# A fused sparse attention and SwiGLU kernel: another order of the same steps, and 39 products on zeros in place of 88

## The chip, the core and the metric

The kernel runs on one NeuronCore of a Trainium2 chip. Five engines work side by side, each through its own queue and strictly in the order of that queue: TensorE (PE: matrix products and transposes), ScalarE (ACT: exponentials, tanh, copies out of PSUM), VectorE (DVE: elementwise work and reductions), GpSimd (POOL: casts, masks, and the issue of some transfers) and SyncE (SP: the issue of the other transfers). They meet through semaphores: an instruction waits in its queue until its inputs are there, and whatever stands behind it waits too. The metric is the time of one execution in microseconds (us).

## The reference

There are two parts. The first is attention over 4 batches, 8 heads, 768 positions and 64 features, in which each query sees only some chunks of 32 keys. For each chunk an upper bound of the score is made from the chunk's smallest and largest key; the 6 best causal chunks are kept; softmax runs over the kept keys. The second part takes the attention's rows (3072 x 512), normalizes them, and applies a gated feed-forward layer of width 1536.

```
k_min, k_max = min, max of k over each chunk
ub    = sum over features of max(q * k_min, q * k_max), causal chunks only
kept  = the 6 chunks with the largest ub, and only keys up to the query
attn  = softmax(q k^T / 8 over the kept keys) @ v
xn    = x / sqrt(mean(x^2) + 1e-6) * rms_g          # x: attn as 3072 x 512
g     = xn @ w_gate
out   = (g * sigmoid(g) * (xn @ w_val)) @ w_out
```

## The kernel before

**Pieces.** Heads are taken in pairs: 16 pairs, four to a batch (pair 0 to 3 is batch 0). The feed-forward layer is done in halves of a batch, 384 rows each, so there are 8 of them. All of it is cut into 1923 steps. A step is one to 32 instructions on one engine. Each step has a name; a text such as "the scores of pair 3" below means all steps `sc` of that pair.

**A pair's path.** SP issues the loads `kload` and `qload` (two transfers each, line 505) into the tiles `knat` and `qnat`; POOL issues the load of v (`vx`, line 481). PE turns k and q (`kT`, `qT`, line 525), three blocks a step; ACT or DVE evicts them (`kE`, `qE`, lines 297 and 301). DVE reduces the chunks (`kmn`, `kmx`, lines 554 and 556), `dif` takes the difference (line 607), `relu` clamps q (line 641 or 643). PE makes the bounds (`ub`, line 731), ACT and DVE evict them (`ubE`), PE turns them back (`up`, line 755), DVE adds the causal mask (`ubm`, line 770), finds the best chunks (`max`, line 658) and writes the selection (`sel`, lines 682 and 687, or 673 and 676 from pair 3 on). For pairs 0 to 2 the selection is turned on PE (`selT`, line 702) and copied by ACT or DVE (`selC`); from pair 3 on SP turns it by two DMA transposes (`qX`, line 565), which wait for `sel` and for a cast of q (`qN`). Casts of k to bf16 (`kC`, `qC`) run on POOL or ACT. Then come twelve scores (`sc`, lines 876 and 882), twelve exponentials on ACT (`exp`, line 893), masks on POOL (`mask`, line 899), twelve products with v (`av`, line 912) and the division on DVE (`xb`, lines 932 and 933). Pair 3 does this in two halves of its queries.

**The feed-forward part.** For each half of a batch, DVE and ACT sum the squares (`sq`), DVE and POOL take the root (`eps`, `root`), DVE scales three rows of blocks (`xs`, line 989). In batch 0 PE turns them (`tp`, line 1011) and ACT or DVE evicts (`tpE`); in later batches SP turns them (`xT`). Then follow twelve `gate` (PE, four products each, line 1045), `tanh` (ACT, line 1052), `tg` (DVE, line 1058), `val` (PE, line 1066), `hh` (DVE, line 1074), and nine `po` (PE, line 1086), whose results are evicted (`poE`) and stored by SP (`out`). The weights come in six transfers that POOL issues: `wg`, `wv` (line 445) and `wo` (line 450), two each.

**Fillers.** 88 further steps, `busy` (line 346), are products of a tile of zeros with itself, into a PSUM bank that nobody reads. 48 of them are 512 columns wide and need only the tile `zeros`, which DVE clears; 40 are 256 wide and may run after the last score of pair 2.

**What sets the order.** Nothing runs while the steps are declared: `order.add` collects them with their dependencies, the buffers that they open and a rank. `Order.run` then plays the program in the kernel's own time model, written out in the source: each engine takes, when it is free, the ready step of the lowest rank whose buffers are free. Ranks are sums of the numbers in `RANK` and `TIMES`. Fillers have the highest ranks, so they are taken where PE has nothing else. Transfers form one line of `load / RATE` each, whichever queue issues them. The order in which steps are taken is the order in which their instructions are emitted, and so the order of every queue; the slot numbers chosen there fix which PSUM bank or SBUF tile a step uses.

```
done = order.run(PLACE)
for s in done:
    s.emit(s.eng)
```

Of the kernel before, what the change touches and what calls it, by code (L numbers as in the profile page):

```python
# [11 lines left out]
ACT = mybir.ActivationFunctionType  # L12
# [13 lines left out]
RANK = (  # L26
    dict(
        av=439.71, dif=-349.0, eps=-276.35, exp=56.9, kC=119.11, kE=221.89, kT=-479.5,
        kload=-91.99, kmn=-561.73, kmx=-221.73, max=-117.69, qC=120.39, qE=644.67, qN=97.14,
        qT=303.27, qX=110.23, qload=17.43, relu=-156.64, root=392.56, sc=392.96, sel=176.91,  # L30
        selC=388.0, selT=-168.59, sq=-325.5, tp=-47.15, tpE=460.17, ub=-387.44, ubE=-1000.64,
        ubm=-238.37, up=-379.03, vload=-360.06, xb=-167.37, xs=293.02,
    ),
    dict(
        av=-243.01, dif=-122.81, eps=-968.41, exp=80.0, gate=-57.45, hh=-33.27, kC=474.21,
        kE=54.78, kT=-28.02, kload=327.35, kmn=571.37, kmx=673.95, mask=-6.85, max=351.72,
        out=-338.93, po=268.25, poE=188.61, qE=-4.14, qN=444.8, qT=271.57, qX=-691.62,
        qload=314.07, relu=202.91, root=-1348.37, sc=-186.72, sel=354.08, sq=285.76, tanh=579.3,
        tg=-259.04, ub=-101.04, ubE=-390.25, ubm=307.49, up=-117.99, val=-52.48, vload=103.56,
        xT=119.23, xb=-299.83, xs=-84.52,  # L40
    ),
)

TIMES = {
# [15 lines left out]
}  # L60


class Buf:
    def __init__(self, kind, sub=None):
        self.kind, self.sub = kind, sub
        self.users, self.slot, self.tile, self.done = 0, None, None, 0.0


class Step:
    def __init__(self, name, occ, rank, emit, deps, opens, uses, load, port):  # L70
        self.name, self.engs, self.occ = name, list(occ), occ
        self.rank, self.emit, self.load, self.port = rank, emit, load, port
        self.deps = [d for d in deps if d is not None]
        self.opens, self.bufs = list(opens), list(opens) + list(uses)
        self.start = self.seen = self.eng = None
        self.left, self.ready, self.next = 0, 0.0, []


class Order:
# [1079 lines left out]
```

## Time and profile before

| | before |
|---|---|
| median of 3 runs | 316.09 us (316.01 to 316.24) |
| the profiled execution | span 314.0 us; its own time is not listed apart from that |
| PE | 308.6 us busy, 98% of the span |
| DVE | 230.7 us, 73% |
| ACT | 194.4 us, 62% |
| POOL | 100.7 us, 32% |
| fillers (line 346) | 88 products, 1.3 to 53.6 us |
| moved by DMA | 35.36 MB, mean 113 GB/s |

Busy time is the union of an engine's instructions. A product's record also covers the stretch in which the next one already runs, so the price of one in a dense row is the distance from start to start. A window of the profile gives the busy time of each engine in a stretch of the span; the timeline gives rows "start, length, engine, line, operation, tiles, count"; the time to landing of a transfer runs from its issue to the semaphore that tells of its end.

### The profile page before, as it was taken

Reading aid. Unit: us, or ns where it says so; the run is one execution under the profiler, and the core shown is the slowest. Engines: PE = TensorE matmul, PEld = TensorE weight load, DVE = VectorE, ACT = ScalarE, POOL = GpSimd, SP = SyncE. Lnnn points to the kernel's source line nnn. Section 1 sums busy time; section 2 is a strip of 40 time slices with the busy share of each in tenths; the row PEclk is TensorE's granted clock in tenths of the full one; section 3 lists DMA queues with packets and bytes.
Section 4 is the critical chain, followed back from the end, with each engine's and each line's share of the span. In section 5 each row is a group of like instructions: output and inputs, shape, how many; then the busy total and the mean of one; then the engine's idle time right before and its main releaser. Section 6 shows DMA issues by size and latency. Waiting matters only on the chain.

```text
span 314.0 us, 7640 instructions
## 1 busy us (share of the span) xinstructions
PE 308.6 (98%) x2844; PEld 196.1 (62%) x2844; DVE 230.7 (73%) x654; ACT 194.4 (62%) x420; POOL 100.7 (32%) x157
## 2 busy tenths in 40 slices
PE   7999999999999999999999999999999999999995
PEld 4567877666566775666667565656666645655542
DVE  7699986888988487967986799879464663873530
ACT  5589987863475987478579654344988823333321
POOL 8666534342353564045357300001522220000000
PEclk9999999999999999999999999999999999999999
DMA  8999989989989898979934640002341045001102
GB/s 171 210 190 178 145 108 207 198 114 143 196 86 199 126 179 152 201 164 222 158 79 61 93 102 0 2 2 52 84 94 59 20 118 150 3 0 65 38 22 111
DMA packets 113301, 35.36 MB, mean 113 GB/s; under 512 B 106224, under 2 KB 110064, under 8 KB 113264
## 3 DMA queue, kind: packets, MB, share of 16 engines
q1 hardware_dynamic: 83152, 26.62, 40.9%
q0 software_dynamic: 28512, 7.87, 25.6%
q10 hardware_dynamic: 1600, 0.39, 0.6%
q8 instruction: 22, 0.36, 0.5%
q14 instruction: 15, 0.12, 0.1%
HBM read 28.57 MB, written 6.29 MB: 111 GB/s over the span
## 4 chain that ended last, share of the span: by engine, by line
PE 97%; DMA 1%; ACTq 0%; ACT 0%; issue 0%
PE gp L1045 20%; PE vp L1066 20%; PE po L1086 20%; PE sc L876 12%; PE av L912 7%; PE busy L346 4%; PE pq L525 4%; PE pk L525 3%; PE ub L789 2%; PE ub L731 2%; DMA qnat<-in_q_dram 1%; PE up L811 1%; PE sc L882 1%; PE up L755 1%; PE tp L1011 0%; ACTq L505 0%
## 5 line engine op out<-in xcount | busy, mean ns | idle before, releaser
L893 ACT ACTIVATE pt<-sc 128x512 bf16<-128x512 f32 (+2 forms) x192 | 88.4, 578 | 10.1 <-PE sc L876 5.3
L1052 ACT ACTIVATE sg<-gp 128x384 bf16<-128x384 f32 x96 | 47.7, 500 | 62.7 <-PE gp L1045 60.0
L1066 PE MATMUL vp<-xT,wv 128*128 128x384 bf16 x384 | 77.0, 326 | 0.0
L1045 PE MATMUL gp<-xT,wg 128*128 128x384 bf16 x384 | 76.2, 326 | 0.0
L1086 PE MATMUL po<-wo,hh 128*128 128x512 bf16 x288 | 69.3, 379 | 0.0
L1058 DVE SCALAR_TENSOR_TENSOR tg<-sg,gp 128x384 bf16<-128x384 bf16 x96 | 52.2, 548 | 21.7 <-ACT sg L1052 19.5
L1074 DVE TENSOR_TENSOR hh<-vp,tg 128x384 bf16<-128x384 f32 x96 | 51.8, 551 | 11.1 <-PE vp L1066 7.3
L1045 PEld LDWEIGHTS <-wg 128*128 128x128 bf16 x384 | 36.8, 98 | 24.5 <-issue 1.0
L1066 PEld LDWEIGHTS <-wv 128*128 128x128 bf16 x384 | 36.9, 98 | 24.1
L876 PE MATMUL sc<-qs,ke 128*128 128x128 bf16 (+5 forms) x420 | 51.4, 251 | 0.0
L1086 PEld LDWEIGHTS <-hh 128*128 128x128 bf16 x288 | 27.6, 98 | 27.5
L301 POOL CAST ke<-kt 64x768 bf16<-64x768 f32 x31 | 26.4, 852 | 36.9 <-ACT kt L297 17.0
L876 PEld LDWEIGHTS <-ke 128*128 128x128 bf16 (+1 forms) x420 | 30.3, 97 | 11.3 <-issue 1.6
L899 POOL TENSOR_SCALAR_AFFINE_SELECT pt<-pt 128x512 bf16<-128x512 bf16 (+1 forms) x48 | 24.4, 527 | 37.6 <-ACT pt L893 37.4
L912 PEld LDWEIGHTS <-pt 128*128 128x128 bf16 x672 | 28.8, 98 | 7.7 <-POOL ke L301 0.6
L912 PE MATMUL av<-vx,pt 128*128 128x65 bf16 x672 | 32.6, 193 | 0.0
L299 ACT ACTIVATE osb<-po 128x512 f32<-128x512 f32 x19 | 11.4, 602 | 21.4 <-PE po L1086 21.4
L346 PE MATMUL busy<-zeros 128*128 128x512 bf16 (+1 forms) x88 | 20.1, 349 | 1.3 <-DVE zeros L341 1.3
L933 DVE TENSOR_TENSOR xb<-av,rden 128x384 bf16<-128x384 f32 (+1 forms) x34 | 18.1, 534 | 1.2
L989 DVE SCALAR_TENSOR_TENSOR xs<-xb,ri,gains 128x512 bf16<-128x512 bf16 x24 | 16.9, 746 | 2.7 <-DMA xT<-xs 2.1
L301 POOL CAST qn<-qnat 128x768 bf16<-128x768 f32 x10 | 8.2, 821 | 31.9 <-DMA qs<-qn 30.7
L481 POOL DMA_DIRECT2D vx<-in_v_dram x16 | 16.8, 1052 | 4.0 <-PE av L912 2.6
(87 smaller groups left out, 303.1 us busy)
## 6 DMA issues: line engine op xcount, KB each, us to landing
out_dram<-osb SPq DMA_DIRECT2D x24, 256.0 KB, 2.2
knat<-in_k_dram SPq DMA_DIRECT2D x30, 192.0 KB, 4.3
qnat<-in_q_dram SPq DMA_DIRECT2D x30, 192.0 KB, 4.8
vx<-in_v_dram POOLq DMA_DIRECT2D x16, 192.0 KB, 4.7
wg<-in_moe_w_gate_dram POOLq DMA_DIRECT2D x2, 768.0 KB, 8.6
wv<-in_moe_w_val_dram POOLq DMA_DIRECT2D x2, 768.0 KB, 7.8
wo<-in_moe_w_out_dram POOLq DMA_DIRECT2D x2, 768.0 KB, 9.9
qs<-qn SPq DMA_TRANSPOSE x26, 3.3
```

The lines of the kernel that those rows point to most:

```text
L301: engine[e].tensor_copy(out_, in_)
L346: nc.tensor.matmul(t[:, 0:n], zeros[:, 0:P], zeros[:, 0:n], start=True, stop=True)
L876: nc.tensor.matmul(t[:, x:x + m, :].rearrange("p a b -> p (a b)"), ke[kk, kb * P:(kb + 1) * P], qs[kk, q0 * P:(q0 + m) * P], start=not tri ...
L893: nc.scalar.activation(out=t[:, 0:nn, :], in_=sc.tile[:, 0:nn, :], func=ACT.Exp, scale=SCALE)
L899: nc.gpsimd.affine_select(out=pt.tile[:, 0:nd, :], in_=pt.tile[:, 0:nd, :], compare_op=ALU.is_ge, fill=0.0, base=0, pattern=[[0, nd], [1, ...
L912: nc.tensor.matmul(av.tile[:, qi - i0, :], pt.tile[:, x, :], VX[c.v.slot][:, hl * NT + kb, :], start=(begin and m == 0), stop=(left[0] == ...
L1045: nc.tensor.matmul(t[:], wg[:, g, hs], XT[b].tile[:, g, cols], start=(g == 0), stop=(g == NP - 1))
L1052: nc.scalar.activation(out=t[:], in_=gp.tile[:], func=ACT.Tanh, scale=0.5)
L1058: nc.vector.scalar_tensor_tensor(out=t[:], in0=sg.tile[:], scalar=1.0, in1=gp.tile[:], op0=ALU.add, op1=ALU.mult)
L1066: nc.tensor.matmul(t[:], wv[:, g, hs], XT[b].tile[:, g, cols], start=(g == 0), stop=(g == NP - 1))
L1074: nc.vector.tensor_tensor(out=t[:], in0=vp.tile[:], in1=tg.tile[:], op=ALU.mult)
L1086: nc.tensor.matmul(po.tile[:], hhs[ht].tile[:, th * P:(th + 1) * P], wo[:, ht, :], start=(ht == 0), stop=(ht == NHT - 1))
```

## The change

The planner is gone. `PROGRAM`, a string of 1874 words, holds the order instead. In each word the letter is the engine (P, A, D, G for POOL, S), the number is the step in the order of declaration, and the numbers behind the colon are the slots of the buffers that the step opens. `Order.run` reads the words. Steps, tiles, buffers, instructions and arithmetic stay as they were, except for three things: the order within every queue; the engine of steps that may run on two (for instance `selC` of pair 0, from ACT to DVE, and a `kC` and `qC` of pair 0); and the fillers: of the 88 steps the string holds the first 39 (numbers 4 to 42), all 512 wide.

```
-RANK = ( ... )
-TIMES = { ... }
+PROGRAM = (
+    "D59 G0 D3 S82:0 P4:0 A2 D1 G64 P5:1 D52 S81 D53 D54 D55 P6:2 G61 G65 S88:1 P7:3 S87 P8:4 G60 G66 S152:2 P9:5 "
+    "P10:6 G67 P85:7 S157:3 G73 P83:0 D86:0 P11:1 P12:2 G71 A84 D95:0 P91:3 D58 S326:4 P13:4 P14:5 A92:1 D57 "
...
+    "S224:0 D110:0 G113:0 P334:4 D330:6 A171:0 P111:7 A328 D172 P332:1 A335:2 D112 P173:3 G339:2 A99 S399:1 P25:5 "
...
+)
-    def run(self, places):
+    def run(self, program):
+        engines = {"P": "PE", "A": "ACT", "D": "DVE", "G": "POOL", "S": "SP"}
         out = []
-        while len(out) < len(self.steps):
...
+        for word in program.split():
+            n, _, slots = word[1:].partition(":")
+            s = self.steps[int(n)]
+            s.eng = engines[word[0]]
+            new = [b for b in s.opens if b.slot is None]
+            for b, x in zip(new, slots.split(",") if slots else (), strict=True):
+                b.slot = int(x)
+            out.append(s)
         return out
...
-    done = order.run(PLACE)
+    done = order.run(PROGRAM)
```

What moves, read from the two orders queue by queue, as far as the prediction speaks of it:

- PE before the first `gate`: the same steps in both (48 `sc`, 48 `av`, 14 `qT`, 12 `kT`, 5 `ub`, 5 `up`, 3 `selT`, 3 `tp`), and 88 fillers before, 39 after. 24 of the 39 stand ahead of the first score. No filler stands behind the first `gate` in either.
- PE from the first `gate` to `kT` of pair 5: before 9 `gate`, 4 `val`, 12 `sc`; after 8 `gate`, 3 `val`, 6 `sc`, 2 `tp`.
- DVE: the clearing of one tile `qn` (step 59) stands ahead of the clearing of `zeros` (step 3). `sel` of pair 4 stood ahead of the squares of batch 0's first half; now it stands behind the three `xs` and behind `eps` of the second half.
- ACT before the first `tanh`: before 9 `qE`, 5 `kE`, 5 `ubE`, 3 `tpE`, 1 `selC`, 1 `qC`; after 12, 6, 4, 2, 0, 0. The rest is the same (48 `exp`, 5 `relu`, 4 `sq`, `ke0`, one `kC`). The third `sq` of batch 0's second half stands between `tpE` and `tanh`, and `eps` of that half waits for it.
- SP: the gains' load moves from ahead of pair 1's loads to behind `qX` of pair 3. Around pair 4: `qX` of pair 4 (twice), then `kload` of pair 5, `qload` and `kload` of pair 7, in both orders.
- POOL: before, v of pairs 0, 1, 3, 2, then `wg`, `wv`, a `root`, `wg`, a `root`, `wv`, v of pair 4. After, v of pairs 0, 1, 3, 6, 2, then `wg`, `wg`, `wv`, the two `root`, v of pair 4, `wv`, v of pair 7, `wo`.

More of the change, by code (lines that the diff above doesn't have):

```diff
@@ L22 @@
 GUARD = 480.0
[L26 to L41, printed above, removed]
-)
-TIMES = {
[15 rows of a table removed]
-}
+PROGRAM = (
[123 rows of a table added]
+)
 class Buf:
@@ L65, in __init__ @@
         self.kind, self.sub = kind, sub
-        self.users, self.slot, self.tile, self.done = 0, None, None, 0.0
+        self.users, self.slot, self.tile = 0, None, None
 class Step:
@@ L74, in __init__ @@
         self.opens, self.bufs = list(opens), list(opens) + list(uses)
-        self.start = self.seen = self.eng = None
-        self.left, self.ready, self.next = 0, 0.0, []
+        self.eng = None
 class Order:
-    RATE = 0.21e6
-    COLD = 4.5
-    TAIL = {"PE": 0.27, "ACT": 0.18, "DVE": 0.14, "POOL": 0.10, "SP": 2.0}
     def __init__(self, slots, limits):
@@ L261, in rank @@
         return r
-    PLACE = {"": 1.0}
-    for i, kinds in enumerate(RANK):
-        for kind, x in kinds.items():
-            PLACE[f"{kind}.{i}"] = x
     const = ctx.enter_context(tc.tile_pool(name="const", bufs=1))
@@ L1124 @@
             ffn(b, half, f"f{b}.{half}", f"pacef{b}.{half}")
-    PLACE.update(TIMES)
-    done = order.run(PLACE)
+    done = order.run(PROGRAM)
     for s in done:
```

95 lines of the change are left out of this document (removed), and 135 rows, old and new, of tables (PROGRAM, TIMES).

## The prediction

> **What bounds the kernel now.** I read the page first: busy shares, slices, and the group of the fillers.
>
> ```profile
> span 314.0 us, 7640 instructions
> ...
> PE 308.6 (98%) x2844; PEld 196.1 (62%) x2844; DVE 230.7 (73%) x654; ACT 194.4 (62%) x420; POOL 100.7 (32%) x157
> ...
> PE   7999999999999999999999999999999999999995
> ...
> PEclk9999999999999999999999999999999999999999
> DMA  8999989989989898979934640002341045001102
> GB/s 171 210 190 178 145 108 207 198 114 143 196 86 199 126 179 152 201 164 222 158 79 61 93 102 0 2 2 52 84 94 59 20 118 150 3 0 65 38 22 111
> ...
> L346 PE MATMUL busy<-zeros 128*128 128x512 bf16 (+1 forms) x88 | 20.1, 349 | 1.3 <-DVE zeros L341 1.3
> ```
>
> PE is never idle. So its queue sets the end, and time goes only if PE gets less to do, or if what it does not do in the first 54 us is not replaced by a wait. PE's waits and the windows of all engines (columns: PE, PEld, DVE, ACT, POOL busy, PEclk, DMA share, GB/s) say how tight that is.
>
> ```profile
> PE busy L346 <- DVE zeros L341: 1.3, 1, 1.3
> PE pq L525 <- DMA qnat<-in_q_dram: 0.3, 1, 0.3
> ```
>
> ```profile
> 5.00:20.00 15.00, 14.66 (x133) 8.77 (x132) 11.59 (x32) 10.37 (x18) 10.81 (x17) 1.00 1.09 208
> 20.00:48.00 28.00, 27.97 (x427) 21.52 (x426) 26.43 (x103) 26.73 (x62) 13.61 (x18) 1.00 1.16 147
> 48.00:54.00 6.00, 6.00 (x68) 4.91 (x66) 4.32 (x11) 4.56 (x12) 2.82 (x4) 1.00 1.19 219
> 54.00:314.00 260.00, 256.23 (x2216) 159.16 (x2214) 184.97 (x500) 151.25 (x329) 69.24 (x104) 1.00 0.59 100
> ```
>
> From 20 to 48 us ACT is busy for 26.73 of 28 and DVE for 26.43: the fillers there cover waits for these two. Ahead of 20 and behind 48 ACT has holes. Behind 54 us PE alone is full.
>
> **The first part: what the fillers cost.** The timeline of PE gives their spacing.
>
> ```profile
> 1.26 2.74 PE L346 MATMUL busy<-zeros 128*128 128x512 bf16 x6 [1.26 <-DVE zeros L341]
> ...
> 19.34 0.43 PE L876 MATMUL sc<-qs,ke 128*128 128x128 bf16 x3
> ...
> 49.77 0.71 PE L346 MATMUL busy<-zeros 128*128 128x256 bf16 x5
> 50.32 0.82 PE L525 MATMUL pq<-ident_f,qnat 128*128 128x128 f32 x6
> ...
> 52.73 1.24 PE L346 MATMUL busy<-zeros 128*128 128x512 bf16 x5
> 53.81 1.46 PE L1045 MATMUL gp<-xT,wg 128*128 128x384 bf16 x8
> ...
> 64.57 0.82 PE L525 MATMUL pk<-ident_f,knat 128*128 128x128 f32 x6
> 65.23 1.46 PE L1045 MATMUL gp<-xT,wg 128*128 128x384 bf16 x8
> 66.53 0.81 PE L1066 MATMUL vp<-xT,wv 128*128 128x384 bf16 x4
> ...
> 307.69 2.54 PE L1086 MATMUL po<-wo,hh 128*128 128x512 bf16 x11
> ```
>
> Five narrow ones take 50.32 - 49.77 = 0.55, or 0.11 us each; five wide ones 53.81 - 52.73 = 1.08, or 0.216 each; the first six at the start stand 0.42 apart (the next instruction starts at 3.79). The change drops 40 narrow (4.4 us) and 9 wide (1.9 us): 6.3 us. Against that, one more `qn` tile is cleared ahead of `zeros`:
>
> ```profile
> 2.52 1.75 DVE L356 MEMSET qn<- 128x896 uint32 x2
> ```
>
> That is 0.8 us by which the first product starts later. If nothing else waits, the first `gate` moves from 53.81 to 53.81 - 6.3 + 0.8 = 48.3. The work behind the first `gate` is the same set of steps, and PE does it without a hole: from 53.81 to 307.69 + 2.54 = 310.23, 256.4 us. The last stretch to the end of the span is 314.0 - 310.2 = 3.8 us (last eviction and store, the same steps). So the end is the time of the first `gate`, plus 256.4, plus PE's new waits behind it, plus 3.8.
>
> **Can ACT and DVE keep up?** ACT first. Up to the first `tanh`, 0.85 us behind the first `gate`, it is busy for 10.37 + 26.73 + 4.56 = 41.7 us.
>
> ```profile
> 9.22 0.84 ACT L297 ACTIVATE qs<-qt 64x768 bf16<-64x768 f32 x1
> 10.77 0.38 ACT L297 ACTIVATE ubs<-ub 96x256 f32<-96x256 f32 x1 [0.71 <-PE ub L731]
> ...
> 12.60 0.87 ACT L297 ACTIVATE qt<-pq 128x384 f32<-128x384 f32 x2 [0.90 <-PE pq L525]
> ...
> 17.67 1.62 ACT L297 ACTIVATE qs<-st 64x768 bf16<-64x768 bf16 x2 [0.17 <-PE st L702]
> 19.19 0.85 ACT L297 ACTIVATE qt<-pq 128x384 f32<-128x384 f32 x2
> 19.93 0.75 ACT L893 ACTIVATE pt<-sc 128x128 bf16<-128x128 f32 x2
> ```
>
> The new order takes from it `selC` (1.62), `qC` (0.84), one `ubE` (0.38) and one `tpE` (about 0.5), and gives it four evictions (0.44 each): 41.7 - 3.3 + 1.7 = 40.1 us. So a `tanh` 5.5 us earlier, at 49.1, leaves ACT from its first eviction (about 5.7) 43.4 us for 40.1 us of work. Before it had 49.
>
> The early stretch decides. The first score starts at 19.34 now, right behind the 1.62 us of `selC` on ACT. In the new order that copy runs on DVE beside ACT; the last thing in front of the scores is then pair 0's cast on ACT, behind `ke0`, `ubE` and two evictions. I put their rows end to end from PE's first transposes (about 5.0, seven cold fillers behind 2.05) and come to 17.4 for the first score, an estimate. From the first `exp` (19.93) to the first `tanh` ACT now has 31.4 us of work and takes 34.7; the new list there is about as long, 31.5. Without any hole the `tanh` comes at 17.5 + 31.5 = 49.0 and the first `gate` at 48.2, where PE alone would put it (48.3). With the hole of 20 to 48 us (28.00 - 26.73 = 1.3) the gate comes at 49.5; with that of 48 to 54 as well (6.00 - 4.56 = 1.4) at 50.9. I take 49.5: the second hole is the tail in which batch 0's norm waits on its own chain, and the new order has two evictions and a `relu` of pair 5 there.
>
> DVE gives a second bound. Its work up to the third `xs` is the 11.59 + 26.43 of the windows and the part of 48 to 54 that ends with this row, and it loses about what it gains (a `max` pair, a `sel` and a `qN` go behind; a `selC`, a `ubE` come in front).
>
> ```profile
> 45.10 0.45 DVE L673 SCALAR_TENSOR_TENSOR qn<-m,ubm 128x288 bf16<-128x288 f32 x1
> 45.47 0.19 DVE L676 TENSOR_SCALAR qn<-m 128x12 bf16<-128x12 f32 x1
> ...
> 50.13 2.07 DVE L989 SCALAR_TENSOR_TENSOR xs<-xb,ri,gains 128x512 bf16<-128x512 bf16 x3
> ```
>
> Some 43 us of work that can start at 0.9 and must stand about 3 us while the first transposes come end no earlier than 47; a transpose and an eviction later it is 48. So PE, ACT and DVE would all be full at once: 48.3 is a floor, not a forecast.
>
> **A wait that takes the place: pair 5's keys.** `sel` of pair 4 stood at 45.10 to 45.66, eight microseconds ahead of the gate. It moves behind `xs` and behind `eps`, which waits for the last `sq`, and so ends some 1.3 us behind the gate. SP issues two transposes of its result, and pair 5's keys queue behind them:
>
> ```profile
> 45.81 3.44 SPq L565 DMA_TRANSPOSE qs<-qn  x2
> 49.30 2.78 SPq L505 DMA_DIRECT2D knat<-in_k_dram  x2
> ```
>
> ```profile
> DMA to landing us min/median/max: 7.4/8.8/10.1
> ```
>
> ```profile
> knat<-in_k_dram SPq DMA_DIRECT2D x30, 192.0 KB, 4.3
> ```
>
> The third row is the time to landing in the window 49 to 52 us, the two transfers of pair 5's keys; the last one is the page's median of all. With the gate at G the transposes issue at G + 1.4, the keys 49.30 - 45.81 = 3.5 later at G + 4.9, the second of the two about 0.7 behind. By the median both are there at G + 9.9; as slow as in the window (the second 10.1 behind its issue) at G + 15.7. PE wants them after 8 `gate` and 3 `val` (two gates take 66.53 - 65.23 = 1.30, so 11 x 0.65), 6 scores and 2 `tp` (about 0.22 each, as a 512-column product), at G + 9.0. Before, the same keys were wanted at 64.57, 10.8 behind the gate. So the wait is between nothing (a load faster than the median) and 6.7 us; the median gives 0.9. I take 1.5, near the median, because the weight load beside which the slow one ran has gone earlier.
>
> ```profile
> 49.24 0.80 POOL L445 DMA_DIRECT2D wg<-in_moe_w_gate_dram  x1
> ```
>
> The new order issues it before the two `root`; what then runs beside the keys is v of pair 4, the second `wv` and v of pair 7.
>
> The Trainium skill, DMA: Bandwidth & Descriptors, section "Issuing engines are not separate DMA queues", says that transfers begun by different engines end up on the same 16 DMA engines and interleave. The trace agrees: the keys took up to 10.1 us beside `wg`, 4.3 as a rule. By that rule POOL's three transfers would slow pair 5's keys again, and the sum would be that of the fourth case below; by the median row it is the forecast.
>
> **The sum.** 49.5 + 256.4 + 1.5 + 3.8 = 311.2 us of span. The median of the runs, 316.09, lies 2.1 above the span; so 313.3 us, 0.9% below. Other moves (gains later, v of pair 6 earlier, the finer mix of `sc`, `av`, `gate`) I cost at nothing: the cover is feed-forward work, and in 54 to 314 ACT is busy for 151 of 260 us and DVE for 185. Where that cover is gone, a wait is paid in full, since PE takes its queue in order.
>
> **The other cases.** What a measurement tells from no change here is about 0.2%, 0.6 us.
>
> First, all three engines stay full and the keys come in time: 48.3 + 256.4 + 3.8 + 2.1 = 310.6. For it: the waits of PE above are 1.6 us in all. Against it: the holes in ACT's windows. 0.2.
>
> Second, the forecast, with 0.7 to 3 us of wait: 312 to 315. 0.35.
>
> Third, the gate comes late, ACT losing what it loses now (50.9, or 52 where early loads are late too): 314.7 to 316. This is also the case in which the change does not do what it says, since the zeros go and PE stands idle in their place. 0.17, half of it within 0.2%.
>
> Fourth, slower: the transposes of pair 4 hold up pair 5's keys, which take as long as in the window 49 to 52. PE waits 6.7 us: 49.5 + 256.4 + 6.7 + 3.8 + 2.1 = 318.5. It decides once the wait is over 53.8 - 49.5 = 4.3 us, that is, once these keys land later than 53.8 + 9.0 = 62.8 us. For it: both slow rows. Against it: the `wg` beside it is gone. 0.23.
>
> Fifth, such a wait slows the clock as well. At the start products stand 0.42 apart instead of 0.216 for about 3.4 us, although PE is busy; as many again would cost 8 x 0.2 = 1.6 us: 320.1. The Trainium skill, TensorE: Matmul & The Clock Gate, section "What's actually happening", has the clock halved after an idle window of about 3.4 us; PEclk shows nothing of it here, since PE is never idle that long. 0.05.
>
> So faster 0.62 (the first two and a part of the third), same 0.1, slower 0.28. The range is 310.0 to 318.5: from PE's sum with the gate some 0.6 earlier to the fourth case. The forecast's own range is 312 to 315.
>
> **What would show it.** In the profile after: the first `gp` row at 49.5 (48.3 to 51); `busy` x39 and about 10 us; the first `sc` row near 17.4; ACT busy for over 27 of 28 us in 20 to 48; a wait of PE on `pk` for the DMA of `knat` near 59 us, of 1 to 3 us; no other wait over 1 us behind it; `po` ending 3.8 us ahead of the span's end. I am wrong on the covers if PE's waits behind 70 us come to more than 1.5 us; wrong on ACT if the gate comes behind 51; wrong on the sign if pair 5's keys land behind 62.8.

## The result: 343.8 us in place of 316.05, and the profile after

The changed kernel takes 343.79 us (median of 4 runs, 342.98 to 345.49) against 316.05 us for the kernel before on the same chip. The ratio is 1.088, with a 95% interval of 1.086 to 1.091. The forecast was 313.3 with a range up to 318.5, so size and sign are both wrong. Times in this document are medians of all executions, ratios and intervals leave out those more than 1.5% above the kernel's fastest, and a profile shows one execution, whose time is given where it lies far from the median. In the rows of the changed kernel the line numbers are 8 lower: `busy` is line 338, the loads 497, the transposes 517, `sc` 868, `gate` 1037; in the runs further below they are 7 to 10 lower.

The page: its span, the busy time of the engines, and the granted clock in 40 slices.

```profile
span 341.7 us, 7415 instructions
...
PE 310.9 (91%) x2770; PEld 196.8 (58%) x2795; DVE 231.7 (68%) x661; ACT 188.8 (55%) x410; POOL 103.3 (30%) x160
...
PEclk9899996797899999999999999999989999999998
```

PE has 49 weight loads (PEld) fewer, one for each product on zeros that is gone; its own count falls by 74 because some 25 records of products are missing from this trace. PE is busy for 91% of the span in place of 98%. The clock, full throughout before, falls in four stretches: near 9 to 17, 51 to 68, 77 to 94 and 247 to 256 us. The timeline of PE has the first `gate`:

```profile
66.63 1.62 PE L1037 MATMUL gp<-xT,wg 128*128 128x384 bf16 x9
```

It stands 12.8 us later than before (53.81); the way from there to the span's end is 275.1 us in place of 260.2. So of the 27.7 us, 12.8 arise ahead of the `gate` and 14.9 behind it. PE's waits (total, times, longest, in us) name the causes:

```profile
PE pq L517 <- DMA qnat<-in_q_dram: 8.6, 3, 7.9
PE pk L517 <- DMA knat<-in_k_dram: 7.2, 2, 4.3
PE av L904 <- POOL pt L891: 3.2, 1, 3.2
PE busy L338 <- DVE zeros L333: 2.2, 1, 2.2
PE av L904 <- DMA vx<-in_v_dram: 1.6, 1, 1.6
```

Before there was one wait for a load, of 0.3 us. The chain of work that ended last, in order of time, holds transfers too. Three of its pieces, the keys of pair 1, the last load of pair 0's queries and a load of pair 5's queries:

```profile
3.43 3.71 DMA knat<-in_k_dram
7.16 4.99 DMA qnat<-in_q_dram
37.89 19.68 DMA qnat<-in_q_dram
```

The third, 19.7 us for half of one pair's queries, is twice the slowest landing that the prediction reckoned with (10.1). Before the change this load and the first weight transfer (`wg`) went out so, first SP, then POOL:

```profile
33.50 2.19 SPq L505 DMA_DIRECT2D qnat<-in_q_dram  x2
38.53 0.79 POOL L445 DMA_DIRECT2D wg<-in_moe_w_gate_dram  x1
```

The queries landed 4.0 to 4.7 us behind their issues, when the first weights set out, and PE wanted them at 50.32. After the change three weight transfers stand around the load, and PE waits:

```profile
36.81 1.51 POOL L437 DMA_DIRECT2D wg<-in_moe_w_gate_dram  x2
37.47 0.97 SPq L497 DMA_DIRECT2D qnat<-in_q_dram  x2
39.96 0.75 POOL L437 DMA_DIRECT2D wv<-in_moe_w_val_dram  x1
57.71 0.87 PE L517 MATMUL pq<-ident_f,qnat 128*128 128x128 f32 x3 [7.88 <-DMA qnat<-in_q_dram]
```

The windows (columns as in the prediction) show the clock beside the waits:

```profile
5.00:20.00 15.00, 11.60 (x100) 6.91 (x98) 9.28 (x29) 6.61 (x12) 9.05 (x17) 0.89 1.22 224
20.00:48.00 28.00, 25.35 (x381) 19.38 (x383) 25.34 (x85) 25.45 (x58) 18.39 (x24) 1.00 1.23 142
48.00:68.00 20.00, 11.90 (x105) 8.26 (x103) 8.73 (x34) 9.56 (x22) 1.79 (x3) 0.74 0.47 82
68.00:100.00 32.00, 25.93 (x217) 17.19 (x216) 20.04 (x47) 15.58 (x34) 13.09 (x19) 0.89 1.17 162
```

PE is idle for 3.4 of 15, 8.1 of 20 and 6.1 of 32 us, and the clock is 0.89, 0.74 and 0.89 there. Of the 8.1 us, 7.9 are the one wait for pair 5's queries.

Two more places can be read from the timelines. The first is the start. The second halves of pair 0's four loads are issued not by SP but by ACT (line 505, after the change 497). ACT's timeline before and after:

```profile
0.80 1.07 ACTq L505 DMA_DIRECT2D knat<-in_k_dram  x2
1.90 1.05 ACTq L505 DMA_DIRECT2D qnat<-in_q_dram  x2
2.98 1.28 ACT L338 ACT_TABLE_LOAD   x1 [2.98 <-issue]
```

```profile
0.80 0.49 ACTq L497 DMA_DIRECT2D knat<-in_k_dram  x1
1.32 1.28 ACT L330 ACT_TABLE_LOAD   x1 [1.32 <-PEq L1134]
2.61 0.20 ACT L330 ACTIVATE first<-ident_f 128x1 f32<-128x1 f32 x1
4.70 0.40 ACTq L497 DMA_DIRECT2D knat<-in_k_dram  x1
5.14 2.39 ACTq L497 DMA_DIRECT2D qnat<-in_q_dram  x2
```

The word `A2` (`first`, the activation that brings ACT's table) stands ahead of three of the four. Before, the four went out between 0.80 and 2.95 us; now the last goes out at 7.16. `first` itself takes only 1.5 us of that. In the chain the last issue stands right behind the landing of pair 1's keys (3.43 + 3.71 = 7.14), so the rest looks like a wait for earlier transfers; why ACT's issue should hang on them was not looked into. The second place is POOL's queue near the end:

```profile
242.01 0.66 POOL L891 TENSOR_SCALAR_AFFINE_SELECT pt<-pt 128x512 bf16<-128x512 bf16 x1
248.65 0.83 POOL L293 CAST qn<-qnat 128x768 bf16<-128x768 f32 x1 [5.98 <-issue]
249.42 0.42 POOL L891 TENSOR_SCALAR_AFFINE_SELECT pt<-pt 128x256 bf16<-128x256 bf16 x1
```

A mask of pair 12 stands behind a cast of pair 15 (`qN`). The profile names no releaser for the 5.98 us before the cast; the cast's buffer is one that DMA transposes read, and the last of these, issued at 241.3, lands 7.1 us later, just before the cast starts. PE waits 3.2 us for the mask.

### The profile page after: what moved, and what is told of

Its sections match the earlier page's. It is cut to its first block, busy times and chain, and to the rows that moved or that the text cites. A ratio compares the mean times of both kernels' runs of the same rounds, so it can differ in the third digit from the quotient of the medians.

```text
span 341.7 us, 7415 instructions
## 1 busy us (share of the span) xinstructions
PE 310.9 (91%) x2770; PEld 196.8 (58%) x2795; DVE 231.7 (68%) x661; ACT 188.8 (55%) x410; POOL 103.3 (30%) x160
## 4 chain that ended last, share of the span: by engine, by line
PE 75%; DMA 12%; DVE 3%; issue 3%; SPq 2%; POOL 2%; ACT 0%; POOLq 0%
PE po L1078 18%; PE vp L1058 17%; PE gp L1037 17%; DMA qnat<-in_q_dram 11%; PE sc L868 8%; PE av L904 5%; PE pq L517 3%; PE pk L517 2%; SPq L497 2%; PE ub L781 2%; PE busy L338 1%; DMA knat<-in_k_dram 1%; DVE m L650 1%; POOL ke L293 1%; PE up L803 1%
## 5 line engine op out<-in xcount | busy, mean ns | idle before, releaser
L885 ACT ACTIVATE pt<-sc 128x512 bf16<-128x512 f32 (+1 forms) x192 | 92.9, 556 | 38.8 <-PE sc L868 36.1
L1037 PE MATMUL gp<-xT,wg 128*128 128x384 bf16 x384 | 73.4, 329 | 0.0
L1066 DVE TENSOR_TENSOR hh<-vp,tg 128x384 bf16<-128x384 f32 x96 | 51.1, 552 | 12.6 <-PE vp L1058 11.5
L868 PE MATMUL sc<-qs,ke 89*128 89x128 bf16 (+5 forms) x419 | 56.3, 255 | 1.8 <-DVE hh L1066 1.5
L904 PE MATMUL av<-vx,pt 128*128 128x65 bf16 x672 | 40.9, 197 | 4.8 <-POOL pt L891 3.2
L904 PEld LDWEIGHTS <-pt 128*128 128x128 bf16 x672 | 35.0, 100 | 16.4 <-POOL pt L891 3.5
L891 POOL TENSOR_SCALAR_AFFINE_SELECT pt<-pt 128x256 bf16<-128x256 bf16 (+1 forms) x48 | 25.0, 531 | 58.6 <-ACT pt L885 54.6
L868 PEld LDWEIGHTS <-ke 89*128 89x128 bf16 (+1 forms) x420 | 31.0, 99 | 12.1 <-issue 3.7
L293 POOL CAST ke<-kt 64x768 bf16<-64x768 f32 x31 | 25.8, 831 | 18.2 <-PE sc L868 10.1
L517 PE MATMUL pq<-ident_f,qnat 128*128 128x128 f32 x96 | 16.4, 292 | 8.6 <-DMA qnat<-in_q_dram 8.6
L517 PE MATMUL pk<-ident_f,knat 128*128 128x128 f32 x96 | 16.6, 292 | 7.3 <-DMA knat<-in_k_dram 7.2
L924 DVE RECIPROCAL rden<-av 128x6 f32<-128x6 f32 (+1 forms) x34 | 6.9, 202 | 21.0 <-PE av L904 20.7
## 6 DMA issues: line engine op xcount, KB each, us to landing
wo<-in_moe_w_out_dram POOLq DMA_DIRECT2D x2, 768.0 KB, 10.1
```

The lines of the kernel that those rows point to most:

```text
L293: engine[e].tensor_copy(out_, in_)
L517: nc.tensor.transpose(t[:, j * P:(j + 1) * P], nat[w].tile[:, j0 + j].rearrange("p h d -> p (h d)"), ident_f[:])
L868: nc.tensor.matmul(t[:, x:x + m, :].rearrange("p a b -> p (a b)"), ke[kk, kb * P:(kb + 1) * P], qs[kk, q0 * P:(q0 + m) * P], start=not tri ...
L885: nc.scalar.activation(out=t[:, 0:nn, :], in_=sc.tile[:, 0:nn, :], func=ACT.Exp, scale=SCALE)
L891: nc.gpsimd.affine_select(out=pt.tile[:, 0:nd, :], in_=pt.tile[:, 0:nd, :], compare_op=ALU.is_ge, fill=0.0, base=0, pattern=[[0, nd], [1, ...
L904: nc.tensor.matmul(av.tile[:, qi - i0, :], pt.tile[:, x, :], VX[c.v.slot][:, hl * NT + kb, :], start=(begin and m == 0), stop=(left[0] == ...
```

## The experiments

Three theories. **Late loads:** transfers are issued late, or starved beside POOL's weights, and each wait costs its length and some clock behind it. **Fewer products on zeros:** with 39 in place of 88, TensorE has too little to do, and its clock falls of itself. **Many small waits:** the finely mixed order costs a little everywhere. All runs compare with the kernel before on the same chip (315.9 to 316.1).

### One cause at a time in the changed kernel

`first` behind all four of pair 0's loads:

```diff
-D59 G0 D3 S82:0 P4:0 A2 D1 G64 ... S88:1 P7:3 S87 P8:4
+D59 G0 D3 S82:0 P4:0 D1 G64 ... S88:1 P7:3 S87 A2 P8:4
```

> The changed kernel (343.8) with one word moved: ScalarE's `first` (the activation that brings its table) stands behind all four of pair 0's loads that ScalarE issues, as before the change, not ahead of three of them. Late loads (each wait on TensorE for a transfer that was issued late or starved is the cause): the four are issued by 3 us and land by 7 in place of 12.1, the second half of `kT@a0` starts near 5 in place of 8.8, `sc` starts near 18 in place of 21.8, and the time falls by 3 to 5 us, to 338.8 to 340.8; the wait of 8 us for pair 5's queries stays. Fewer products on zeros (the clock falls because TensorE has too little to do): the number of products is the same, so 343 to 345. Many small waits of the finely mixed order: 342 to 344, at most 2 us.

Measured: 332.25 us, four executions from 327.69 to 336.41, ratio 1.043 (1.037 to 1.049). By the median that is 11.5 us less than the changed kernel, by the ratio (329.3 us) 14.5: more than twice what was expected. The profile is of an execution of 333.62 us. Its waits and one window:

```profile
PE pk L515 <- DMA knat<-in_k_dram: 6.5, 2, 5.5
PE pq L515 <- DMA qnat<-in_q_dram: 4.5, 3, 4.0
```

```profile
48.00:68.00 20.00, 16.79 (x135) 11.10 (x136) 12.41 (x38) 12.69 (x27) 8.03 (x11) 0.91 0.70 106
```

The first score starts at 17.82 in place of 21.77, so 4 us come back at the start, as expected. But the wait for pair 5's queries, which was expected to stay, halves (7.9 to 4.0): all goes 4 us earlier, these queries are issued at 33.5 and take 16.1 us in place of 20.1 from the first issue to the last landing. The clock between 48 and 68 rises from 0.74 to 0.91 with it. The first `gate` stands at 57.46, 9.2 us earlier, of which 4.0 arise before the first score and 3.9 at this wait. In this profile a late start cost its own length and as much again.

Pair 5's queries right behind pair 4's:

```diff
-... S539:4 A121:2 ... P540:5 S469:6 P214 ...
+... S539:4 S469:6 A121:2 ... P540:5 P214 ...
```

> The changed kernel (343.8) with one word moved: the load of pair 5's queries stands on SyncE right behind the load of pair 4's (S539), ahead of the three weight transfers of GpSimd's queue in place of beside them. Late loads: it lands 10 us earlier or more, the wait of 8.0 us at `qT@a5` goes (under 1 us is left), the clock granted between 48 and 68 us is above 0.85 in place of 0.74, the first gate row is at 55 to 59 in place of 66.6 and the time falls by 8 to 11 us, to 333 to 336. Fewer products on zeros: TensorE has as little to do as ever, so 341 to 345 and the clock still falls. Many small waits: the wait breaks up into others, 339 to 343.

Measured: 331.74 us, ratio 1.050 (1.046 to 1.055), 1 us under the range of the first theory. Pair 5's queries are no longer waited for, the clock in 48 to 68 us is 0.97, the first `gate` at 55.1. The next late load is longer than before, pair 5's keys:

```profile
PE pk L515 <- DMA knat<-in_k_dram: 9.8, 2, 6.8
```

The second and third weight transfer later instead:

```diff
-... G75 ... G77 ... G548:1 ... G76 ... G1233:4 G1322:0 ...
+... G75 ... G548:1 ... G76 G1233:4 G77 G1322:0 ...
```

> The changed kernel (343.8) with two words moved: the second and third weight transfers of GpSimd's queue are issued just ahead of the gate's own steps, not beside the load of pair 5's queries. Sharing packet by packet (the load's 1536 packets of 256 bytes take turns with the weights' packets of 1536 bytes): with one weight transfer left beside it, the load takes 8 to 12 us in place of 20.1, the wait at `qT@a5` falls from 8.0 to under 2, and the time by 5 to 10 us, to 334 to 339, less what the gate then waits for its weights (0 to 4). If the load is slow for another cause (late issue, or the queue of SyncE itself): it takes 16 us or more still, and the time is 342 to 347.

Measured: 332.68 us, ratio 1.056 (1.050 to 1.061), again about 1 us under the range. The load of the queries is issued in the same place and takes 11.8 us (median of its two halves) in place of 16.8, and PE waits 0.5 us for it; so what is beside it counts, and not only when it is issued. Part of the gain goes back at the gate, where PE now waits for a weight, and 3.0 us go to pair 7's queries:

```profile
PE gp L1036 <- DMA wg<-in_moe_w_gate_dram: 4.8, 1, 4.8
PE pq L516 <- DMA qnat<-in_q_dram: 3.5, 2, 3.0
```

`qN` of pair 15 behind two masks:

```diff
-... P1126:0,5 ... P1562:7 ... G1123:1 P1128:6 ... G1012 ... G1029 ...
+... P1126:0,5 ... P1562:7 ... P1128:6 ... G1012 ... G1029 G1123:1 ...
```

> The changed kernel (343.8) with one word moved: GpSimd's `qN` of pair 15 behind the two masks of pair 12 that stood after it. Head of the queue (the mask waits because the copy ahead of it waits for a transfer of 7 us): the wait of 3.2 us of `av` for GpSimd's `pt` falls below 0.5 and the time by 2.5 to 3.5 us, to 340.3 to 341.3, if nothing else is late there. If other work fills the time anyway: 343 to 344.5.

Measured: 340.43 us, ratio 1.075 (1.071 to 1.079): 3.4 us less, and `av` no longer waits for `pt`. A word on a queue that is 30% busy was worth 1% of the time. Up to 240 us the order is that of the changed kernel, and yet the wait for pair 5's keys is 6.4 us here in place of 4.3; single waits differ by that much between executions.

v of pairs 6 and 7 later:

```diff
-... G353:2 ... G551:3 ... G78 ... G569:0 ... G79 ... G491:2 ...
+... G353:2 ... G78 ... G79 G551:3 ... G491:2 G569:0 ...
```

> The changed kernel (343.8) with only v of pairs 6 and 7 moved to the same later places. Late loads: v of pair 6 no longer stands beside the loads of pairs 4 and 6 at 25 to 34 us, v of pair 7 no longer beside the keys of pair 5 and the queries of pair 7; the wait of 8.0 us for pair 5's queries falls by 1 to 3 us and that of 4.4 for pair 5's keys by 1 to 3, and the time by 2 to 6, to 338 to 342. If only the transfers right beside a load count, and these are the weights: 342.5 to 344.5.

Measured: 344.94 us, ratio 1.090 (1.088 to 1.093): nothing gained, 0.4 above the range of the second account, which holds for pair 5's queries: their wait stays (8.4). The wait for pair 5's keys does go, but 3.7 us come back at pair 4's `qX` and 2.6 at pair 7's queries, which now meet the weights. Where one load is sped up, another is late.

### One cause at a time in the kernel before

The first 39 products only:

```diff
-        s.emit(s.eng)
+        if s.name != "busy" or id(s) in kept:
+            s.emit(s.eng)
```

> The kernel before (316.1) with the first 39 products on zeros of its 88 and nothing else changed. Late loads (the products on zeros only cover time in which TensorE would wait): each product taken away turns into waiting of the same length, the first gate row stays at 53 to 55 and the time at 314 to 318. The prediction's own reckoning (the products cost their time): 6 us go, 309 to 311. Fewer products as the cause of the loss (idle time takes TensorE's clock): the granted clock between 5 and 50 us falls below 0.9 and the time rises by 5 us or more, to 321 or above.

Measured: 317.6 us (10 executions), ratio 1.005 (1.003 to 1.007). They fall into two groups: three at 315.8 to 315.9 us, where the granted clock is full, and seven at 317.4 to 318.3, where its mean is 0.989 to 0.995. The profile shows one of the three. Its clock is full in all 40 slices, and the first `gate` stands where it stood (53.57 in place of 53.81):

```profile
53.57 4.06 PE L1045 MATMUL gp<-xT,wg 128*128 128x384 bf16 x24 [1.04 <-ACT xT L297]
```

PE is busy for 5.2 us less (303.4 in place of 308.6) in the same span (314.1). So the products' time became waits, and the first item of the prediction's sum falls: 49 products fewer save nothing. The number of products explains 1.5 of the 27.7 us by the ratio and 2.5 in the slowest execution; as the main cause the second theory falls. What is true in it is that with fewer products the clock is lost in most executions, for 2 us or so; no profile shows where.

`first` ahead of three of ACT's loads, and nothing else:

```diff
+    one, two = order.steps[2], order.steps[81]
+    done.remove(one)
+    done.insert(done.index(two) + 1, one)
```

> The kernel before (316.1) with one word moved: ScalarE's `first` ahead of three of the four loads that it issues, as the change puts it; all else, the 88 products on zeros too, as before. Late loads: the three are issued 3.5 to 4.5 us later, `kT@a0`'s second half starts 3.5 to 5 us later and the first gate row too, and the time rises by 3 to 6 us, to 319 to 322. If the start has slack that the products on zeros or the later loads give back: 316 to 317.5.

Measured: 323.44 us, ratio 1.023 (1.021 to 1.024). More than the 3 to 6 us expected: one word costs a kernel with all its products 7.4 us, the wait and then the clock:

```profile
PE pk L525 <- DMA knat<-in_k_dram: 5.0, 1, 5.0
```

```profile
5.00:20.00 15.00, 9.95 (x66) 5.78 (x66) 4.68 (x11) 5.54 (x9) 4.57 (x10) 0.77 0.96 188
```

### How a load is starved

While the changed kernel waits, the window from 44 to 56 us shows the two queues at work, POOL's (q0) and SP's (q1); columns: packets, MB, share of the 16 engines:

```profile
q0 software_dynamic: 1400, 2.00, 91.9%
q1 hardware_dynamic: 1351, 0.34, 21.2%
```

They move almost equally many packets, but POOL's are mostly of 1536 bytes and SP's of 256: the queries get one seventh of the bytes. In stretches of 2 us it is nearly one for one: 234 and 233 from 46 to 48, 228 and 229, then 227 and 228. The Trainium skill, DMA: Bandwidth & Descriptors, section "Queues, rings and completion order", says that each DMA engine goes round its queue rows packet by packet. The trace agrees in the turns; the page's packet holds some 9 to 17 descriptors, and how that relates to the packets counted here no run shows.

This is not the whole of the 20 us. From 38 to 43 us SP's queue is still passing 128 packets of 2 KB, the gains' load, which the change put right ahead of these queries; their own packets come in number only behind it. What that move costs by itself was not tested.

Two kernels of transfers alone test it:

```
for each case: alone, beside 2 loads of v, beside 3 weights, beside the same weights cut in four
    nc.gpsimd.dma_start(...)       # the case's transfers
    nc.sync.dma_start(out=qt[:, :, hl, :], in_=q[1, 2 + hl]...)   # two halves
```

> A kernel of transfers alone, whose output holds nothing of the reference's: SyncE loads one pair's queries (two transfers of 128 x 6 x 64 floats, packets of 256 bytes) four times, each time once the transfers before have landed: alone; beside two of GpSimd's v loads (packets of 128 bytes in the source); beside three of its weight transfers (128 x 4 x 768, packets of 1536 bytes); and beside the same weights cut into transfers of 192 columns (packets of 384 bytes). Sharing packet by packet: 3.5 to 5 us alone, 6 to 9 beside v, 15 to 20 beside the weights, 7 to 10 beside the cut weights. Sharing by bytes: 3.5 to 5, 6 to 7, 6 to 8, 6 to 8. First in, first out on the 16 engines (the load stands behind what is queued): beside the weights and the cut weights alike, 10 to 16.

> The kernel of transfers alone once more, with the load of the queries issued some 2 to 4 us behind GpSimd's transfers, not a little ahead of them, in all four cases; its output again holds nothing of the reference's. First of the two halves, from issue to landing: alone 2.7 as there. Sharing packet by packet: 8 to 12 beside the weights, 4 to 6 beside the cut weights, 3.5 to 6 beside v. By bytes, or first in first out: beside the weights and the cut weights within 1.5 us of each other.

In the first kernel the load went out ahead of the weights. One half took 2.5 to 2.7 us in all cases; the other took 2.9 alone, 9.2 beside the weights, 4.7 beside the cut ones. None of its accounts has these numbers. The second kernel's issues (last number: median us to landing of the two halves):

```profile
q_alone<-in_q_dram SPq DMA_DIRECT2D x2, 192.0 KB, 2.9
...
q_beside_w<-in_q_dram SPq DMA_DIRECT2D x2, 192.0 KB, 11.8
q_beside_wcut<-in_q_dram SPq DMA_DIRECT2D x2, 192.0 KB, 9.0
```

The load is four times as slow beside the weights as alone, and the same bytes in smaller packets hurt it less, in both kernels. The counts say why: from 26 to 32 us, beside the whole weights, POOL's queue passes 224, 238 and 226 packets in stretches of 2 us and the load 225, 238 and 226, though a packet of POOL's has six times the bytes. That rejects sharing by bytes, and a strict first in, first out. The cut weights hurt more than was expected (9.0, expected 4 to 6): in both cases the load's first packets move only some 3.7 us behind its issue (1.1 alone), and what holds them that long was not tested. Nor are the two cases alike in all else, since POOL issues the twelve cut transfers over 9 us and the three whole ones over 2. The v transfers had nearly passed when the load's first packets moved (3.2), so that case shows nothing.

### Does work on zeros hold the clock?

36 more products on zeros inside the wait for pair 5's queries, all in one bank:

```diff
-... A369:4 P470:4 ...
+... A369:4 P43:4 ... P51:4 P285:4 ... P311:4 P470:4 ...
```

> The changed kernel (343.8) with 36 more products on zeros just ahead of `qT@a5`, that is inside the wait of 8.0 us for pair 5's queries: 75 products in place of 39, no load earlier. If the idle wait itself takes TensorE's clock behind it (0.74 granted between 48 and 68 us): the clock stays above 0.9 there, the transposes behind the wait take 0.33 in place of 0.65, and the time falls by 1.5 to 3 us, to 341 to 342.5, though TensorE has 8 us more to do. If the clock falls for another cause: the clock stays at 0.74 and the time is 343 to 345.

Measured: 347.63 us, ratio 1.100 (1.097 to 1.104), 3.8 us slower than without, and outside both accounts. Windows from 52 to 64 us of the changed kernel, and then of this one:

```profile
52.00:56.00 4.00, 0.00 (x0) 0.00 (x0) 0.00 (x0) 0.00 (x0) 0.62 (x1) 0.66 1.07 186
56.00:60.00 4.00, 2.29 (x14) 2.16 (x15) 0.42 (x1) 0.98 (x2) 0.00 (x0) 0.50 0.11 18
60.00:64.00 4.00, 3.78 (x35) 2.57 (x35) 2.19 (x7) 2.76 (x6) 0.00 (x0) 0.56 0.00 0
```

```profile
52.00:56.00 4.00, 3.40 (x11) 0.95 (x10) 0.30 (x3) 0.08 (x1) 0.89 (x1) 1.00 1.11 193
56.00:60.00 4.00, 3.38 (x12) 1.17 (x12) 0.00 (x0) 0.00 (x0) 0.00 (x0) 0.84 0.23 41
60.00:64.00 4.00, 3.50 (x10) 0.94 (x9) 0.00 (x0) 0.00 (x0) 0.00 (x0) 0.50 0.00 0
```

In the changed kernel PE stops at 49.8 and the clock is at half from about 53.3 to 63.5 (0.66 of a window of 4 us is 1.3 us at full clock and 2.7 at half; 0.56 is 0.5 at full), so it fell 3.5 us into the idle time. PE has work again from 57.7; 5.8 us at half clock cost 2.9 us. The Trainium skill, TensorE: Matmul & The Clock Gate, section "What's actually happening", has it halved after an idle window of some 3.4 us; these rows agree. In the second table PE's records fill 3.4 of 4 us and the clock falls all the same, only later. These products, all in one bank, stand 0.39 us apart on average (first at 50.5, last at 64.1, 36 of them) where a dense row has 0.11 for the narrow ones. So they ran some 6 us past the time at which the queries land without them (57.7), and the clock was lost as well. That the clock falls behind idle time is shown by the first table and by `first` in the kernel before, where PE has no product from 5.1 to 10.1 and the clock is at half from 8.5 to 15.3; that thinly set products do not hold it is seen here once, and why was not tried further.

### All loads mended together

`first`, pair 5's queries and `qN` of pair 15 as above, the loads of pair 5's keys and pair 7 ahead of the weights:

```diff
-... S539:4 ... S352 ... S351 ... S464:0 ... S557:5 ... S552:1 ...
+... S539:4 S469:6 S464:0 ... S352 ... S351 S557:5 S552:1 ...
```

> The changed kernel (343.8) with the order of the loads alone mended, all on the queues: ScalarE's `first` behind its four loads; the loads of pair 5's queries and keys right behind pair 4's queries (S539), those of pair 7 behind the queries of pair 3 on their way to tokens (S351), all ahead of the weights; and GpSimd's `qN` of pair 15 behind the two masks that stood after it. No product on zeros is added and no step of TensorE, VectorE or ScalarE's arithmetic moves. Late loads: the waits for `qnat` and `knat` fall below 1 us in sum behind 10 us, the granted clock is 0.98 or above between 48 and 100 us, the first gate row stands at 52 to 54, and the time is 315 to 321, so at least 22 of the 27.7 us come back. Fewer products on zeros: the clock stays at 0.9 or below in one of these stretches and the time above 328. Many small waits of the finely mixed order: the waits for loads go and 323 to 330 is left, spread over waits under 1 us each.

Measured: 326.54 us, ratio 1.032 (1.029 to 1.034). A miss: 17.3 of 27.7 us come back, not 22 or more. The time lies in the range of the third theory, but not its account, many waits under 1 us. The waits for queries and keys fall to 1.1 us in all, and a new one has come, with the clock at 0.85 and 0.86 in the windows from 20 to 48 and 48 to 68:

```profile
PE sc L866 <- DMA qs<-qn: 9.5, 4, 5.3
```

The keys of pair 5 now stand ahead of pair 3's `qX` on SP's queue and delay its issue by 2.6 us, into the weights; there a DMA transpose takes 9 to 14 us in place of 3 to 4. Three words back:

```diff
-... S539:4 S469:6 S464:0 ... S351 S557:5 S552:1 S74 ...
+... S539:4 S469:6 ... S351 ... S74 S464:0 S557:5 ...
```

> The mended order of loads (326.5), mended once more: the loads of pair 5's keys and pair 7's queries stand behind `gains`, no longer ahead of pair 3's queries on their way to tokens (`qX`), and pair 7's keys where the change puts them. All else is the changed kernel with `first`, pair 5's queries and `qN` of pair 15 moved as there. Late loads: `qX` of pair 3 is issued at 30 in place of 32.7, lands before the weights start and its waits of 9.5 us and the clock lost with them (2 to 2.5) go; the first gate row is at 51 to 53 and the time 313 to 317. If pair 5's keys are then starved beside the weights and come late themselves: 317 to 321. Fewer products on zeros, or many small waits: 321 or above with no wait over 1 us behind 20 us.

Measured: 320.24 us, ratio 1.014 (1.012 to 1.016), in the range of the second account. But pair 5's keys are in time. The profile is of an execution of 325.6 us, while the other four took 319.7 to 320.8. In it the first `gate` is at 51.5, as expected, and the wait for `qs` is again 9.8 us in all, 8.8 of it at pair 4's `qX`, which now meet the weights and v of pair 4; in the other four it must be shorter. With the second and third weight later too:

```diff
-... G75 ... G77 G548:1 ... G76 ... G406 ... G549:0 ...
+... G75 ... G548:1 ... G406 G77 ... G549:0 G76 ...
```

> The same with two words more: the second weight transfer behind GpSimd's `dif` G406 and the third behind `qN` of pair 6, so that v of pair 2 and pair 5's keys have one weight transfer beside them, not three. Late loads, shared packet by packet: v of pair 2 lands 1 to 3 us earlier and its wait goes, 0.5 to 2 us faster than without; but a weight that comes late puts a wait of 0 to 3 us at the gate: 312 to 318. If sharing plays no part: the same time as without these two words, within 0.5 us.

Measured: 321.07 us, ratio 1.016 (1.014 to 1.018): 0.8 slower, outside both accounts; the wait for `qs` is 5.5. The next two leave the first three weights as in the run of 320.24 us. They move v of pairs 6 and 7 back, and then `qN` of pair 5 ahead of v of pair 4 and of the fourth weight:

```diff
+... G79 G551:3 ... G491:2 G569:0 ...
+... G479:1 G421:1 G78 ...
```

> The order of loads mended twice (320.2), with v of pairs 6 and 7, which are issued near 22 and 56 and first used near 119 and 107, put behind the first part of the last projection's weights and behind v of pair 5 on GpSimd's queue, so that 384 KB less stand in the queues up to 68 us. Late loads (the transfers up to 60 us fill the queues, and each order only chooses which one is late): pair 4's queries on their way to tokens (`qX`, issued at 53 and 55, 8 to 10 us beside the rest) land in under 5 us, TensorE's waits for `qs` fall from 9.8 (5.5 in the kernel with spread weights) to under 3 and the time to 311 to 316. If it is the lateness of `qX`'s issue alone, not what runs beside it: the waits stay over 5 and the time is 318 to 321.

> The same with GpSimd's `qN` of pair 5 ahead of v of pair 4 and the next weight transfer, not behind them; as that copy waits until pair 4's `qX` have landed, these two transfers no longer run beside them. Late loads: `qX` of pair 4 lands in 2.7 to 4 us, as where the queues are empty, its wait goes (under 1 us), and the time is 0 to 3 us under the kernel without this, 309 to 314. If v of pair 4 or the weights then come late: the wait moves to `av` or `vp`, and the time is 314 to 319.

Measured: 318.08 us (ratio 1.005, 1.003 to 1.008) with the first line and 317.4 (1.005, 1.002 to 1.008) with both, twelve executions each. The first lies between its two accounts: a time at the edge of the second, but in its profile, of 321.15 us, a wait for `qs` of 4.3. In the second run's profile (316.96 us) that wait is 1.0, and the wait has moved to `av`, as its second account has it:

```profile
PE av L902 <- DMA vx<-in_v_dram: 2.7, 2, 1.7
...
PE sc L866 <- DMA qs<-qn: 1.0, 2, 0.5
```

The clock is full in all 40 slices of this profile; in five of the twelve executions, of 319.5 to 321.0 us, its mean is still 0.989 to 0.995, and in six of the twelve without the last line. Against the changed kernel nine words out of 1874 have moved, none of them arithmetic on TensorE or VectorE, and 26.4 of the 27.7 us are back, with 39 products on zeros as in the changed kernel. A last run moved five transfers away from the two waits for v:

```diff
+... G406 G77 ... G549:0 G76 ... G449 G78 G79 G551:3 ...
```

> The order of loads mended three times (317.4; span of its profile 315.2, in which v of pairs 2 and 4 are still waited for, 1.7 and 1.0 us), with five transfers of GpSimd's queue moved so that nothing large runs beside these two: the second and third weight transfer behind `dif` G406 and `qN` of pair 6, and the fourth, the first of the last projection and v of pair 6 behind the first mask of pair 4. Late loads: both waits fall below 0.5 and the time by 1.5 to 3 us, to 314.5 to 316, level with the kernel before or a little under it. If other work covers them, or a weight comes late at the gate: 317 to 319.

Measured: 317.23 us, ratio 1.005 (1.003 to 1.006), in the range of the second account. The waits for v stay at 2.4. What it brings is steadiness: all ten executions have a clock of 0.998 or more and take 316.4 to 319.0 us. In this profile the first `gate` stands at 51.9, 1.9 us earlier than before the change, and from there to the end of the span (315.0) it takes 263.1 in place of 260.2. So the mixed order gains 1.9 ahead of the `gate` and gives back 2.9 behind it. Of these 2.9, the waits for v are a part; whether the rest belongs to the mix itself was not settled, and no order tried here beats the kernel before.

## Why the prediction was wrong, step by step

**What bounds the kernel now.** "Time goes only if PE gets less to do, or if what it does not do in the first 54 us is not replaced by a wait" was right as a sentence and applied wrongly. The 6.3 us for 49 products was a saving that did not exist: taken away alone they brought nothing in three executions of ten and cost some 2 us in seven. A filler that is taken where nothing else is ready costs nothing, and its price from start to start is no gain.

**The first score at 17.4.** It came at 21.77. The list of ACT's work was nearly right, since with `first` behind the loads the score starts at 17.82. What was left out is that ACT issues four of pair 0's transfers, and that `first` was moved ahead of three of them. The diff showed it in its first line.

**The gate at 49.5.** It came at 66.6, 17.1 later: 4.4 from the first score, 7.9 from the wait for pair 5's queries, and 4.8 that no row splits further, the lost clock among them. With the loads mended it stands at 51.1 to 52.0. That is where the prediction put its third case (50.9 to 52), so ACT's holes were not filled either: in the last run it is busy for 25.65 of the 28 us from 20 to 48, where over 27 were forecast.

**The wait for pair 5's keys, 1.5 us (0 to 6.7).** It is there and took 4.3. The load landed 8.8 and 10.1 us behind its issues, so the slow row was the right one and not the median; the fourth case had this wait at 6.7. The failed sentence is "because the weight load beside which the slow one ran has gone earlier". Gone earlier, it ran beside pair 5's queries. Their load had been 11 us early before the change, and the sum gave it no term at all. This is the step that decides: 7.9 us of wait and the clock behind it.

**The clock, a case with 0.05 and 1.6 us.** Four stretches lost clock, the last behind the wait of 3.2 us for a mask (0.84 from 245 to 256). Beside a wait of 5.0 us, the one-word run lost 2.4 us more. This case should have gone along with each long wait, not been a case of its own; near 3 us it can go either way, since a wait of 3.0 us in the run with late weights (75 to 78 us) left the clock full.

**"Other moves I cost at nothing".** The cover was named as feed-forward work, which lies on PE, ACT and DVE; nothing of it covers a mask behind a cast on POOL, and that cost 3.4 us. One of these moves, the gains' later load, put 256 KB right ahead of pair 5's queries on SP's queue.

**The tail.** 275.1 in place of 256.4 + 3.8 behind the `gate`, from 4.3 (keys), 3.2 (mask), 1.5 (a score behind `hh`) and the lost clock with smaller waits.

The rival that came nearest in kind is the fourth (starved behind the weights), with its sign and mechanism, but for one load and 6.7 us of wait. In fact the start, two loads of pair 5 and a mask came late, and the clock fell behind each.

## What to carry to other kernels

When an order is rewritten, first list every transfer with its issue, its landing and its first use, what stands ahead of it on its own queue, and what is issued beside it on the others; a load that was 11 us early is as much at risk as one that was just in time. Price a filler by what it covers, and price each wait of several microseconds with the clock behind it. Look for instructions that issue transfers on engines that are counted as compute engines.

## What the runs showed of the hardware

The two queues took turns packet by packet: 1351 packets of 256 bytes passed beside 1400 of mostly 1536 bytes. A load that takes 2.9 us alone took 11.8 beside three weight transfers, of which some 3.7 passed before its first packets moved. DMA transposes suffer likewise, from 3 to 4 us up to 14. Waits of 5.0 and 7.9 us took 2 to 3 us of clock with them (7.4 - 5.0 = 2.4, and 2.9 above). 36 products 0.39 us apart in a single bank did not hold the clock, although the records call PE busy for 3.4 of 4 us. With fewer products on zeros the kernel before also became less steady: 315.8 to 318.3 over 10 executions, against 315.5 to 316.2 with all 88 in the same session.
